# Sixteen products of ones instead of ten at the start of a fused attention, soft-MoE and GLU kernel, and another order for its attention stage

## The chip, the core and the metric

The kernel runs on one core of one Trainium2 chip. The core has TensorE (matrix products, called PE in the profile, with its weight loads as PEld), VectorE (DVE), ScalarE (ACT), GpSimd (POOL) and SyncE (SP), which here only issues DMAs. Each engine runs its own instruction list in order and waits for the others by semaphores. The metric is the device time of one launch in microseconds (us), as the median over runs. Before the change it is 510.9 us over 3 runs (509.9 to 510.99).

## The reference

Three layers follow each other, all in float32:

- causal attention over `q, k, v` of shape (4, 12, 448, 64): scores times 1/8, mask above the diagonal, softmax, times `v`. The result is laid out as `x` of 1792 tokens by 768;
- a soft mixture of 8 experts: `logits = x @ phi` (32 slots, 4 for each expert); softmax over the tokens gives the input of each slot, `d.T @ x`; each expert computes `relu(slot @ w1) @ w2` on its 4 slots (768 to 1024 to 768); softmax over the slots mixes the 32 results back to the tokens, `c @ slot_out`;
- a gated layer: `sigmoid(x @ w_gate) * (x @ w_val) @ w_out` (768 to 1536 to 768).

The weights of the experts are 50 MB, those of the gated layer 14 MB.

## The kernel before, in words

**Attention (0 to some 217 us).** The 48 heads are taken in 24 pairs; two pairs share one of 12 groups of loads (`q`, `k`, `v` of four heads, on SP's queue; the first `k` on ACT's). For a pair `i` the steps are: `T` (TensorE turns the rows of `q` and `k` into columns, tile `psT`), `hi` (ACT) and `lo` (DVE), which split them into two float16 parts (`qT`); `S` (scores in three products, `psS`), `m` (DVE: mask and row minimum), `e` (ACT: exponential, `P`), `pt` (TensorE transposes `P` into `psP`), `C` (ACT or DVE copies it to `PT`), `V` (times `v`, `psV`), `xu`, `Xa`, `xn` (back to rows), and for two pairs together `Y`, `yt`, `U`, `Ur`, `Ul` (logits; `Ul` is POOL's sum into `ln`). After each six pairs a tail (`psl`, `bm`, `eT`, `pse`, `A`, ...) folds the batch into the running softmax over the tokens. The scale of a group comes from its sums of squares: for groups 2 to 11 POOL squares (`sq`, two halves for `q` and two for `k`) and adds up in five halving steps (`add`, tiles `sq` and `sqr`), then TensorE spreads the sums over the partitions (`psq`) and DVE makes the scale (`sc`), which `hi` needs. In groups 0 and 1 DVE and ACT do the squares.

In the same stretch the first two weights of the gated layer are loaded and converted from their 64-bit words (`cv`: for each of six blocks two steps on ACT and two on DVE, tiles `w` and `first`), and expert weights are loaded ahead into nine buffers.

**The order is planned at build time.** `Plan` (L20 to L98) holds every step with its engines and an assumed length. `play` first goes backwards and gives each step a due time: that of its successor, less the successor's length times `slack`, less `margin`. Then it adds a constant for each kind of step from the table `SHIFT`. Then it goes forwards: of the steps that can start on the engine that is free first, within `wait` of the earliest, it issues the one with the smallest due time. What it issues is fixed: `on.te` and the rest (`Pinned`) keep the engines' program order. So at run time an engine never overtakes; it waits for the step that the plan put next. The times of the plan are not seen by the chip.

**Products of ones.** `keep_warm` (attention) multiplies a 128x128 tile of ones by two copies of itself into a spare bank (`psf`), and nobody reads it. The steps `("fs", n)` issue two such products each; they have an earliest time in the plan (`first=`) and a due time, so they are put where TensorE would be idle in the plan. `NFIRST` is their number. More products of ones (`("fl", k)`) stand in the last tail and ahead of the gated layer.

**Experts (217 to some 297 us).** The expert weights come in on SP's queue in tiles of 1.5 MB, four for each expert. Attention's memory is given back tile by tile, and five more buffers for weights (`w2p`, `w2px`) lie there. TensorE takes the experts in turn (`psh`, `psht`, `so`).

**Gated layer (to the end).** Six units of 256 columns, ordered by a second `Plan` with its own numbers (`SLACK`, `MARGIN`, `WAIT`, `GSHIFT`).

Of the kernel before, what the change touches and what calls it, by code (L numbers as in the profile page):

```python
# [19 lines left out]
class Plan:  # L20
# [5 lines left out]
    def op(self, key, f, on, deps=(), new=(), use=(), behind=(), due=1e9, first=0.0, lag=0.0, mode=""):  # L26
        for r, x in new:
            self.tiles[x] = [len(self.ops)]
        for x in use:
            self.tiles[x].append(len(self.ops))  # L30
        n = SimpleNamespace(key=key, f=f, on=on, deps=[self.at[x] for x in deps], new=list(new),
                            behind=[self.at[x] for x in behind], due=due, first=first, lag=lag, mode=mode, end=None, e=None)
        self.at[key] = len(self.ops)
        self.ops.append(n)

    def chained(self, x, key):
        was = self.last.get(x)
        self.last[x] = key
        return [was] if was else []
# [62 lines left out]
def kernel(  # L102
# [14 lines left out]
    B, H, S, D = q.shape  # L117
# [19 lines left out]
    for b in range(B):  # L137
        h = 0
# [5 lines left out]
    for g, (b, h0, n) in enumerate(GRP):  # L144
        for o in range(0, n, 2):
# [12 lines left out]
    NV = 2  # L158
    E0 = 6
    NH = 8  # L160
    NFIRST = 25
    LAND = (2.0, 5.5, 9.5)
    LDT = 3.9
    SLACK, MARGIN, WAIT = 0.213, 0.838, 0.347
# [22 lines left out]
    NFILL = 20  # L187
    AE = 9
    SQN = 32
    ASLACK, AMARGIN, AWAIT = 0.573, 1.325, 0.083  # L190
    PERIOD = 7.8
    SHIFT = {('A', 0): -67.34, ('A', 1): 96.11, ('C', 0): 69.6, ('C', 1): 119.07, ('C', 2): 112.34, ('C', 3): 125.19,
# [9 lines left out]
             3): -174.56, ('mr',): -54.03, ('p4',): -1.12, ('phi',): -95.42, ('pse',): -29.83, ('psl',): 20.96,  # L202
# [4 lines left out]
    XNB = 6  # L207
    PB = (0, 4, 2, 2)

# [5 lines left out]
    first = bctx.enter_context(tc.tile_pool(name="first", side="right", bufs=1)).tile([128, 2, KC, UC], F32, name="first")  # L215
# [123 lines left out]
    with ExitStack() as actx:  # L339
# [23 lines left out]
        P = {(t, h): P_p.tile([128, 128 * (t + 1)], F32, name=f"P{t}{h}") for t in range(NQ) for h in range(2)}  # L363
# [37 lines left out]
        xu = [x_p.tile([128, 512], F32, name=f"xu{n}") for n in range(2)]  # L401
        yt = x_p.tile([128, 512], F32, name="yt")
# [405 lines left out]
        op = pa.op  # L808
        plain = lambda f, *a: lambda e: f(*a)
# [142 lines left out]
                        k += 1  # L952

        for n in range(NFIRST):
            op(("fs", n), plain(keep_warm, n, 2), {"P": 0.21}, [], first=3.0 + 0.28 * n if n < 5 else 6.6 + 0.33 * (n - 5), new=[] if n else [("p", ("fs",))], use=[("fs",)] if n else [],
               behind=[("fs", n - 1)] if n else [])
        for n in range(NC + NA + NV):
            op(("w", n), lambda e: load_w(), {"D": 1.3}, [("cv", n - NC - NA, z, 3) for z in range(3)] if n >= NC + NA else [], lag=6.5,
               first=19.0 + 15.3 * n)
# [4 lines left out]
        for g_ in range(NG):  # L964
            group(g_)
            for i in range(2 * g_, 2 * g_ + 2):
                pair(i)
                if i % NPB == NPB - 1:
                    tail(i // NPB)
        pa.shift = SHIFT  # L970
        pa.play()
# [120 lines left out]
    for e in range(E):  # L1092
        if e == 0:
            hm = hm0
        else:
            ps = ps1.tile([128, 256], F32, tag="a", name="psh")
            for kc in range(KC):
                w = wt["1", e, kc // 3]
# [3 lines left out]
            hm = hm_p.tile([128, 256], F32, tag="hm", name="hm")  # L1102
            relu_own(hm, ps, e)
        pt = ps1.tile([128, 2, 128], F32, tag="b", name="psht")
# [4 lines left out]
        for f in range(8):  # L1109
            g, i = divmod(f, 2)  # L1110
            w = wt["2", e, f // 4]
# [4 lines left out]
        if e < B:  # L1116
# [3 lines left out]
            c = call[:, b]  # L1120
# [20 lines left out]
    pt = ps1.tile([128, 2, 96], F32, tag="b", name="psst")  # L1141
# [84 lines left out]
    op, chained, last = pl.op, pl.chained, pl.last  # L1226
# [37 lines left out]
    first = len(pl.ops)  # L1264
    prep(0)
    for n in range(NFILL):
        op(("fl", n), lambda e, n=n: keep_warm(n), {"P": 0.11}, [("fl", n - 1)] if n else [(psg, 0)], new=[] if n else [("o0", ("fl",))],
           use=[("fl",)] if n else [], due=10.0)
# [3 lines left out]
    for u in range(NU):  # L1272
        if 0 < u < NU - 1:
            prep(u + 1)
        for b in range(B):
            for c in range(2):
# [7 lines left out]
                   use=[("hs",) + k])  # L1284
# [3 lines left out]
        for i in range(TT):  # L1288
            bs = sorted({t // S for t in (128 * i, 128 * i + 127)})
            k = (u, i)  # L1290
            c = 1.95
            now += c + 0.51
            los, his = ([(f, b, u, c_) for b in bs for c_ in range(2)] for f in (hlo, hhi))
            new = [("o0", ("o0",) + k), ("o1", ("o1",) + k)]
# [5 lines left out]
            else:  # L1300
                op((outp,) + k, lambda e, k=k: outp(*k), {"P": c}, los + ([(wlo, u)] if u else []),
                   new=new, use=[("hid", b, u) for b in bs], behind=chained("out", (outp,) + k), due=now)
            for n in range(2):
                call = lambda f, n=n, k=k: lambda e: f(*k, n, *([e] if f is evict else []))
                e = {"A": 0.5, "V": 0.53} if u == 0 else {"A": 0.5} if u < NU - 1 and (n == 0 or i % 3 == AE and u < 4) else {"V": 0.53}
                a = u > 0 and "A" in e
# [40 lines left out]
```

## Time and profile before

| what | value |
|---|---|
| median of 3 runs | 510.9 us (509.9 to 510.99) |
| the profiled execution, own time | 510.54 us |
| its span, first to last instruction | 508.7 us |
| PE busy | 475.8 us (94%) |
| DVE, ACT, POOL busy | 379.8, 340.3, 283.7 us |
| mean granted TensorE clock | 0.989 |

An engine's busy share is a mean over three stages with different limits, so the stages are read one by one. Matrix products are pipelined and their ends are modelled: neighbours overlap in the rows, and the time from one start to the next tells the pace. A row of the timeline gives the start, the time from the first start to the last end, the engine, the line, the operation, the tiles and the number of instructions merged; in brackets is the idle time before it and who ended it. SPq and ACTq are the issues of DMAs. Nearly all instructions carry line 248, the helper `Pinned`, so they are told apart by their tiles.

### The profile page before, as it was taken

What the parts mean: (1) busy time and instruction counts of PE and PEld (TensorE: products, weight loads), DVE (VectorE), ACT (ScalarE), POOL (GpSimd) and SP (SyncE); (2) the same over time, 40 slices, a digit from 0 to 9 for tenths busy, and PEclk for the clock granted to TensorE, in tenths of its full rate; (3) what the DMA queues carried; (4) which work ended last, traced back from release to release, by engine and by line L of the source; (5) the groups of instructions that cost most, each with busy time, mean ns of one, the idle gap of its engine ahead of it and who ended that gap; (6) DMA issues with size and microseconds to landing.
All of it is one profiled execution on the core that took longest, in us unless ns stands there. A gap on an engine that the chain in (4) does not pass through costs nothing.

```text
span 508.7 us, 12285 instructions
## 1 busy us (share of the span) xinstructions
PE 475.8 (94%) x4614; PEld 297.9 (59%) x4614; DVE 379.8 (75%) x928; ACT 340.3 (67%) x772; POOL 283.7 (56%) x372
## 2 busy tenths in 40 slices
PE   8999999999999999999874678999999999999996
PEld 6676766677676767665441334555555555555553
DVE  4889999999999998522106039897998998988564
ACT  4899998888887977301131049899878989677410
POOL 3179778778878832000000005548799898998610
PEclk9999999999999999999995999999999999999999
DMA  9766685567765556789999995450353610200144
GB/s 189 195 155 198 184 225 133 162 200 209 212 147 161 167 162 251 300 341 414 421 421 421 412 398 222 171 201 1 125 206 118 247 51 1 91 35 1 57 193 186
DMA packets 84796, 101.56 MB, mean 200 GB/s; under 512 B 65024, under 2 KB 66176, under 8 KB 82688
## 3 DMA queue, kind: packets, MB, share of 16 engines
q1 hardware_dynamic: 84256, 100.32, 58.4%
q8 instruction: 36, 0.59, 0.5%
q10 hardware_dynamic: 480, 0.46, 0.3%
q14 instruction: 24, 0.20, 0.1%
HBM read 95.26 MB, written 5.51 MB: 198 GB/s over the span
## 4 chain that ended last, share of the span: by engine, by line
PE 56%; POOL 15%; DVE 9%; DMA 7%; ACT 6%; issue 5%; SPq 1%; POOLq 0%; ACTq 0%; DVEq 0%
PE pso L248 16%; PE psP L248 6%; PE psS L248 6%; PE psV L248 6%; POOL hlo L248 5%; DMA w<-in_moe_w_dram 5%; POOL sq L248 5%; POOL oacc L248 5%; PE so L1113 4%; PE psT L248 4%; PE psh L1100 3%; PE psY L248 2%; DVE psS L248 2%; PE psX L248 2%; PE psg L248 2%
## 5 line engine op out<-in xcount | busy, mean ns | idle before, releaser
L248 POOL TENSOR_TENSOR hlo<-hs,hhi 128x448 f16<-128x448 f32 x48 | 71.7, 1504 | 111.6 <-ACT hhi L248 111.2
L248 PEld LDWEIGHTS <-hhi 128*128 128x128 f16 x672 | 64.9, 98 | 50.2 <-issue 7.2
L248 ACT ACTIVATE P<-psS,nm 128x384 f32<-128x384 f32 (+3 forms) x168 | 82.2, 507 | 17.1 <-DVE nm L248 13.8
L248 PE MATMUL pso<-wh,hhi 128*128 128x384 f16 x336 | 83.1, 326 | 1.1 <-DVE oacc L248 0.4
L248 PE MATMUL pso<-wl,hhi 128*128 128x384 f16 x336 | 82.4, 326 | 0.0
L248 POOL TENSOR_TENSOR oacc<-oacc,ev 128x384 f32<-128x384 f32 x56 | 75.9, 1371 | 10.8 <-ACT ev L248 10.6
L248 PE MATMUL pso<-wh,hlo 128*128 128x384 f16 x336 | 81.4, 326 | 0.0
L248 DVE SCALAR_TENSOR_TENSOR w<-w 128x1536 int32<-128x1536 int32 (+1 forms) x36 | 69.3, 1926 | 0.4 <-ACT w L248 0.3
L248 DVE CUSTOM_DVE_ANT_0 psS<-psS,cmaskq,sc 128x128 f32<-128x128 f32 (+2 forms) x144 | 62.9, 488 | 1.9 <-PE psS L248 1.2
L248 DVE SCALAR_TENSOR_TENSOR oacc<-pso,osc,oacc 128x384 f32<-128x384 f32 x84 | 49.7, 611 | 18.5 <-PE pso L248 18.3
L248 POOL TENSOR_TENSOR sq<-sq 112x512 bf16<-112x512 bf16 (+1 forms) x80 | 55.3, 691 | 6.3
L248 ACT ACTIVATE w<-w 128x1536 int32<-128x1536 uint16 (+3 forms) x42 | 57.3, 1382 | 1.3 <-DMA w<-in_moe_w_gate_dram 1.3
L248 PE MATMUL psP<-ident,P 128*128 128x128 f32 x384 | 54.6, 278 | 0.3 <-ACT PT L248 0.3
L248 PEld LDWEIGHTS psP<-ident,P 128*128 128x128 f32 x384 | 42.0, 141 | 14.0 <-DVE nm L248 3.5
L248 PE MATMUL psS<-qT,qT 64*64 64x256 f16 (+3 forms) x1008 | 48.3, 287 | 0.7 <-ACT P L248 0.4
L248 PE MATMUL psV<-PT,v 128*64 128x448 f32 (+3 forms) x384 | 46.8, 386 | 0.0
L248 PEld LDWEIGHTS <-hlo 128*128 128x128 f16 x336 | 32.8, 98 | 23.6 <-POOL hlo L248 1.6
L248 ACT COPY PT<-psP 128x512 f32<-128x512 f32 x67 | 38.8, 600 | 3.7 <-PE psP L248 2.6
L248 ACT ACTIVATE ev<-pso,osc 128x384 f32<-128x384 f32 x56 | 32.3, 580 | 13.3 <-PE pso L248 9.6
L337 DVE TENSOR_SCALAR hm<-psh,emask 128x256 f32<-128x256 f32 x8 | 5.3, 663 | 45.8 <-PE psh L1100 43.3
L248 PEld LDWEIGHTS psV<-PT,v 128*64 128x64 f32 x384 | 25.4, 136 | 22.5 <-issue 14.0
L1108 ACT COPY hT<-psht 128x256 f32<-128x256 f32 x8 | 3.0, 372 | 50.6 <-PE psht L1106 43.8
(229 smaller groups left out, 863.6 us busy)
## 6 DMA issues: line engine op xcount, KB each, us to landing
w<-in_moe_w_dram SPq DMA_DIRECT2D x31, 1536.0 KB, 10.3
w<-in_moe_w_val_dram SPq DMA_DIRECT2D x6, 1536.0 KB, 10.7
w<-in_moe_w_gate_dram SPq DMA_DIRECT2D x6, 1536.0 KB, 6.6
w<-in_moe_w_out_dram SPq DMA_DIRECT2D x6, 1536.0 KB, 14.1
out_dram<-oacc SPq DMA_DIRECT2D x13, 384.0 KB, 2.3
k<-in_k_dram SPq DMA_DIRECT2D x44, 112.0 KB, 3.8
q<-in_q_dram SPq DMA_DIRECT2D x44, 112.0 KB, 3.4
v<-in_v_dram SPq DMA_DIRECT2D x36, 128.0 KB, 3.3
```

Of the source, the lines that this page charges most:

```text
L248: x = f(*a, **kw)
L337: nc.vector.tensor_scalar(to.rearrange("s (i q) -> s q i", i=2), ps.rearrange("s (q i) -> s q i", i=2), 0.0, emask[:, e:e + 1], ALU.max, A ...
L1100: nc.tensor.matmul(ps[32 * g:32 * g + 32, :], lhsT=slotT[:, kc, :], rhs=w[:, kc % 3, 256 * g:256 * g + 256], start=kc == 0, stop=kc == KC - 1)
L1108: nc.scalar.copy(hT, pt)
L1113: nc.tensor.matmul(so[32 * c:32 * c + 32, :], lhsT=hT[:, i, 32 * g:32 * g + 32], rhs=w[:, f % 4, 256 * c:256 * c + 256], start=e == 0 and ...
```

## The change

Three things change in the source.

1. `NFIRST` goes from 25 to 28, and the `fs` steps have other earliest times: the first eight (before: five) stand at 2.1 + 0.28 n us of the plan (before: 3.0 + 0.28 n), the other twenty at 6.6 us and every 0.33 us from there, as before. Each step issues two products, so sixteen instead of ten stand ahead of the first `T`.
2. The three numbers that steer attention's plan: `ASLACK`, `AMARGIN`, `AWAIT`.
3. The table `SHIFT`, nearly every entry, with the kinds `("c", 4)` added and `("e", 1)` and `("ld", 2)` dropped.

The steps, their assumed lengths, their dependencies and the buffers stay. The gated layer's plan and numbers stay. No step is added but the six products.

```diff
-    NFIRST = 25
+    NFIRST = 28
...
-    ASLACK, AMARGIN, AWAIT = 0.573, 1.325, 0.083
+    ASLACK, AMARGIN, AWAIT = 1.506, 2.13, 0.08
     PERIOD = 7.8
-    SHIFT = {('A', 0): -67.34, ('A', 1): 96.11, ('C', 0): 69.6, ('C', 1): 119.07, ('C', 2): 112.34, ('C', 3): 125.19,
...
-             152.24, ('c', 0): -12.82, ('c', 1): -9.48, ('c', 2): -10.23, ('c', 3): 64.35, ('cv', 0): -62.16, ('cv',
-             1): -28.45, ('cv', 2): 30.33, ('e', 0): -34.97, ('e', 1): -15.43, ('e', 2): 35.49, ('e', 3): 38.11,
-             ('eT',): -1.33, ('en',): 18.63, ('fl',): 61.86, ('fo',): 29.75, ('fs',): 8.52, ('h',): 21.02, ('hi', 0):
...
-             ('psq', 0): 5.55, ('psq', 2): -1.83, ('psq',): -70.09, ('pt', 0): -171.81, ('pt', 1): 89.79, ('pt', 2):
...
+    SHIFT = {('A', 0): -19.86, ('A', 1): 77.08, ('C', 0): 101.58, ('C', 1): 233.14, ('C', 2): 176.59, ('C', 3): -0.44,
...
+             ('bm',): 6.26, ('c', 0): -41.99, ('c', 1): -134.23, ('c', 2): -5.01, ('c', 3): 40.02, ('c', 4): 2.74,
+             ('cv', 0): -20.38, ('cv', 1): -0.86, ('cv', 2): 17.78, ('e', 0): -0.36, ('e', 2): 112.83, ('e', 3):
+             50.65, ('eT',): -9.25, ('en',): -16.92, ('fl',): 83.37, ('fo',): -9.93, ('fs',): 4.09, ('h',): 18.53,
...
+             0.02, ('mr',): -17.55, ('p4',): -37.61, ('phi',): 92.15, ('pse',): 9.98, ('psl',): -4.74, ('psq', 0):
+             22.0, ('psq', 2): -40.02, ('psq',): 160.93, ('pt', 0): 36.44, ('pt', 1): -25.77, ('pt', 2): 158.6, ('pt',
...
         for n in range(NFIRST):
-            op(("fs", n), plain(keep_warm, n, 2), {"P": 0.21}, [], first=3.0 + 0.28 * n if n < 5 else 6.6 + 0.33 * (n - 5), new=[] if n else [("p", ("fs",))], use=[("fs",)] if n else [],
+            op(("fs", n), plain(keep_warm, n, 2), {"P": 0.21}, [], first=2.1 + 0.28 * n if n < 8 else 6.6 + 0.33 * (n - 8), new=[] if n else [("p", ("fs",))], use=[("fs",)] if n else [],
                behind=[("fs", n - 1)] if n else [])
```

## Rows read from the trace of the kernel before

**Rows 1.** The page's busy times: engine, us, share of the span, instructions.

```profile
PE 475.8 (94%) x4614; PEld 297.9 (59%) x4614; DVE 379.8 (75%) x928; ACT 340.3 (67%) x772; POOL 283.7 (56%) x372
```

**Rows 2.** Stages: window, length, busy us by engine, granted clock, DMA share, GB/s.

```profile
25.00:50.00 25.00, 25.00 (x299) 17.12 (x295) 23.60 (x71) 24.12 (x71) 21.15 (x35) 1.00 0.68 180
...
225.00:235.00 10.00, 10.00 (x134) 5.38 (x131) 2.71 (x8) 1.44 (x3) 0.00 (x0) 1.00 1.03 431
...
270.00:280.00 10.00, 5.89 (x51) 2.44 (x50) 5.29 (x9) 2.11 (x4) 0.00 (x0) 0.54 1.02 423
280.00:300.00 20.00, 13.89 (x181) 7.26 (x182) 2.64 (x7) 1.33 (x4) 0.00 (x0) 1.00 1.01 409
...
400.00:508.00 108.00, 103.84 (x651) 59.94 (x649) 83.88 (x129) 64.78 (x103) 76.09 (x58) 1.00 0.26 96
```

**Rows 3.** Chain of waits that ended last, 190 to 330 us: start, us, what.

```profile
206.23 1.76 PE psV L248 x14
...
217.66 2.73 PE psh L248 x48
...
269.29 25.04 DMA w<-in_moe_w_dram
```

**Rows 4.** SP's queue, 217 to 221 us.

```profile
219.16 1.67 SPq L248 DMA_DIRECT2D w<-in_moe_w_dram  x2
```

**Rows 5.** Stages again, 4 us each, around the end of attention.

```profile
212.00:216.00 4.00, 3.62 (x64) 2.69 (x63) 2.69 (x12) 1.04 (x5) 0.58 (x2) 1.00 1.02 421
216.00:220.00 4.00, 4.00 (x60) 3.01 (x62) 1.60 (x6) 0.00 (x0) 0.00 (x0) 1.00 0.60 250
```

**Rows 6.** Timeline of the first 24 us, all engines.

```profile
1.16 2.31 PE L248 MATMUL psf<-ones 128*128 128x256 bf16 x10 [1.16 <-POOL ones L234]
...
4.56 1.76 PE L248 MATMUL psT<-ident,q 112*64 112x112 f32 x16 [1.08 <-DMA q<-in_q_dram]
...
6.37 1.76 PE L248 MATMUL psT<-ident,k 112*64 112x112 f32 x16
...
7.24 0.61 ACT L248 ACTIVATE qT<-psT,qks 128x448 f16<-128x448 f32 x1
...
8.06 1.46 PE L248 MATMUL psf<-ones 128*128 128x256 bf16 x6
8.17 0.63 ACT L248 ACTIVATE qT<-psT,qks 128x448 f16<-128x448 f32 x1 [0.32 <-PE psT L248]
...
8.84 0.68 DVE L248 SCALAR_TENSOR_TENSOR qT<-psT,qks,qT 128x448 f16<-128x448 f32 x1 [0.23 <-ACT qT L248]
...
9.38 1.08 PE L248 MATMUL psf<-ones 128*128 128x256 bf16 x8
...
10.39 1.26 PE L248 MATMUL psS<-qT,qT 64*64 64x256 f16 x30
...
11.58 0.99 PE L248 MATMUL psT<-ident,k 112*64 112x112 f32 x16
```

**Rows 7.** Stages of 8 us, 20 to 212 us: the sum over them.

```profile
sum 192.00, PE 189.07 PEld 132.78 DVE 176.18 ACT 160.10 POOL 132.15; mean PE 7.88 PEld 5.53 DVE 7.34 ACT 6.67 POOL 5.51
```

**Rows 8.** TensorE's waits, 17 to 217 us: total us, times, longest.

```profile
PE psq L248 <- POOL sqr L248: 1.6, 3, 0.6
PE psS L248 <- ACT P L248: 0.4, 1, 0.4
```

**Rows 9.** Timeline, 46.9 to 50.9 us: POOL's adds and a conversion on DVE.

```profile
46.94 3.80 POOL L248 TENSOR_TENSOR sq<-sq 112x512 bf16<-112x512 bf16 x4
...
47.38 1.27 DVE L248 SCALAR_TENSOR_TENSOR first<-w 128x512 int32<-128x512 int32 x1
```

**Rows 10.** Timelines: the same adds at 75.5 us; PE behind those at 46.94.

```profile
75.52 2.80 POOL L248 TENSOR_TENSOR sq<-sq 112x512 bf16<-112x512 bf16 x4
...
51.11 0.19 PE L248 MATMUL psq<-sqr,avgb 112*128 112x64 bf16 x1 [0.53 <-POOL sqr L248]
```

**Rows 11.** DVE's conversions: ns min/median/max, first and last start us.

```profile
L248 DVE SCALAR_TENSOR_TENSOR w<-w x6: 668/868/1266, 40.5 to 83.9; 128x512 int32<-128x512 int32 x6
L248 DVE SCALAR_TENSOR_TENSOR first<-w x6: 808/1032/1267, 47.4 to 91.9; 128x512 int32<-128x512 int32 x6
```

More of the change, by code (lines that the diff above doesn't have):

```diff
@@ L189 @@
     SQN = 32
-    ASLACK, AMARGIN, AWAIT = 0.573, 1.325, 0.083
+    ASLACK, AMARGIN, AWAIT = 1.506, 2.13, 0.08
     PERIOD = 7.8
-    SHIFT = {('A', 0): -67.34, ('A', 1): 96.11, ('C', 0): 69.6, ('C', 1): 119.07, ('C', 2): 112.34, ('C', 3): 125.19,
[9 rows of a table removed]
-             3): -174.56, ('mr',): -54.03, ('p4',): -1.12, ('phi',): -95.42, ('pse',): -29.83, ('psl',): 20.96,
[4 rows of a table removed]
+    SHIFT = {('A', 0): -19.86, ('A', 1): 77.08, ('C', 0): 101.58, ('C', 1): 233.14, ('C', 2): 176.59, ('C', 3): -0.44,
[9 rows of a table added]
+             0.02, ('mr',): -17.55, ('p4',): -37.61, ('phi',): 92.15, ('pse',): 9.98, ('psl',): -4.74, ('psq', 0):
[4 rows of a table added]
     XNB = 6
```

18 rows, old and new, of the table SHIFT are left out of this document.

## The prediction

> **What bounds the kernel now.** I read the page's busy times first, then the table of stages, then the chain of waits, and last the timeline of the one stage that the edit touches. The busy times put TensorE at 94% of the span [rows 1]; the reader is not to stop there, since the stages differ [rows 2]. In attention TensorE is busy all the time (25.00 of 25 us from 25 to 50 us). Among the experts it is not: from 270 to 300 us it is busy for 19.8 of 30 us while the DMA engines move 409 to 423 GB/s at a share of 1.0, and the chain names a transfer of expert weights there, 25.04 us long [rows 2, 3]. In the gated layer TensorE is the bound again (103.84 of 108 us).
>
> The question is whether attention's end reaches the end of the kernel through the stretch that the DMA bounds. It does. The stream of weights has a hole just where attention ends: the share is 1.02 from 212 to 216 us and 0.60 from 216 to 220 us, because buffers come free only when the first expert's product `psh` (217.66 us) has read them; the next two issues stand at 219.16 us [rows 3 to 5]. From there the stream is without a hole, its bytes are given, and the gated layer starts when it is through. So a microsecond won ahead of 217 us is a microsecond won at the end, and one lost is lost. In the hole the DMA engines stood for 40% of 4 us, 1.6 us: up to that much, the transfers ahead of it do not stop an earlier start either.
>
> **The change part by part.**
>
> *The six more products.* Ten products of ones take 2.31 us, from 1.16 us on, and TensorE then stands until the first rows of `q` have landed, 4.56 us, with 1.08 us of idle [rows 6]. The pace is 2.31/10 = 0.23 us or a little less for each, so six more take 1.39 us at most: sixteen end at 3.47 + 1.39 = 4.86 us, 0.30 us after the first `T` starts now. Products overlap by their ends, so the delay of `T` lies between 0 and 0.30 us; I take 0.1, because the next product does not wait for the last one's end. The cover for the other 1.1 us is the idle before `T`; if `q` landed earlier, all of the six would count.
>
> What they may bring stands in the same rows. Six products of ones at 8.06 us take 1.46 us, eight of the same at 9.38 us take 1.08 us; sixteen products of `T` take 1.76 us at 4.56 and at 6.37 us and 0.99 us at 11.58 us [rows 6]. [...] The granted clock reads 1.00 in attention [rows 2]; of the opening the durations tell more. TensorE had worked without a stop since 4.56 us when the pace rose, and the stop before it was that 1.08 us. The change closes this stop: work is then unbroken from 1.16 us, 3.4 us sooner. If unbroken work is what raises the clock, the rise comes up to 3.4 us earlier, near 6 us, and the second `T` (6.37 us) already runs in 0.99 us instead of 1.76.
>
> The working with an early rise: the second `T` ends near 6.4 + 0.1 + 0.99 = 7.5 us instead of 8.13. Its `hi` on ACT then waits no longer for `T` but for the `hi` ahead of it, 7.24 + 0.61 = 7.85 us, where it starts at 8.17 us now: 0.32 us. The second `lo` on DVE, 8.84 to 9.52 us now, is next: its predecessor on DVE ends at 8.61 us (7.93 plus 0.68 of its like), so it starts 0.23 us sooner and ends near 9.3 us. The first scores could start there. At present they could start at 9.5 us but start at 10.39, because the fourteen products of ones ahead of them (2.4 us at mixed pace) are not through [rows 6]. At the upper level fourteen take some 14 x 1.08/8 = 1.9 us from 7.5 us on, to 9.4 us, and the scores start near 9.4 us: 1.0 us sooner. Up to 17 us the later steps hang on each other through ACT and DVE, with more products of ones between, so most of it should pass on. I take 0.9 us gained, with the bounds +0.3 (the clock rises no sooner, `T` later by the whole 0.30) and -1.8 (a second score step freed in the same way: 2 x 0.9).
>
> [...]
>
> *The order.* Lengths and steps stay, so TensorE's work is the same, and a new order can only change its idle time and the hidden stalls between unlike products. In the 192 us from 20 to 212 us TensorE is idle for 192.00 - 189.07 = 2.9 us [rows 7]. More than half is one kind: `psq` waits for POOL's sums three times, 1.6 us in all [rows 8]. Order alone could win at most about those 2.9 us and a little of what the modelled ends hide, and it could lose as much or more. I take 0.8 us gained, half of what `psq` waits, and for this reason: the larger `AMARGIN` and `ASLACK` bring every step's due time forward by 0.8 us and 0.93 of a length more for each step behind it, so the long chains (load, squares, sums, `psq`, scale, `hi`, `lo`, scores) gain most against short ones, and POOL's sums are the chain that is late now. The table of shifts covers this with up to 280 us of its own for single kinds, and of those I can say no sign. Bounds: -4 (all 2.9 us and a third more hidden in stalls) and +4 (the mirror of it).
>
> The other edits of the table (the converted weights, the loads of weights, which have earliest times of their own, and `phi`) are costed at nothing: ACT, DVE and POOL have 192 - 160.10, 192 - 176.18 and 192 - 132.15 us free in the same stretch [rows 7]. DVE's 16 us are thin cover, and the first rival below takes them away.
>
> *Sum.* -0.9 - 0.8 = -1.7 us on the profiled execution's 510.54 us gives 508.8. That execution lies 0.4 us under the median of the runs, so the median comes to 509.2 us.
>
> **The rivals.**
>
> *Slower: the sums of squares come late more often.* Four of POOL's adds take 2.80 us at 75.52 us and 3.80 us at 46.94 us; in the second case a conversion on DVE, `first<-w`, lies over them, itself 1.27 us where the shortest of these takes 0.668, and `psq` is then idle for 0.53 us [rows 9 to 11]. Of ten `psq` three wait now [rows 8]. If the new order lays the twelve conversions over more of the adds, or puts `psq` further ahead on TensorE's list, those that now come free also wait: six more at 0.6 us are 3.6 us, and 510.54 - 0.9 + 3.6 = 513.2, as a median 513.6 us. It decides from the point at which more than four `psq` wait beyond today's three (4 x 0.6 = 2.4, more than the 0.9 of the start by over 1 us). Against it: the conversions are only 12, all between 40 and 93 us, and seven of ten sums are in time. For it: the table moves `psq` by up to 231 us and gives no word of POOL's real pace.
>
> [...]
>
> *No gain at the start.* The clock rises as late as now, or ACT and DVE, which the early scores then wait for, give the time back before 20 us. The start is then worth 0 and the order is small: 510.0 to 511.8 us as a median, at 510.9 without either. For it: from 11 to 17 us products of ones still fill TensorE, so it is not what is late there.
>
> *The order is worth more.* If most of the 2.9 us go and the stalls between unlike products shrink as well, -3.5 and -0.9 give 506.1, as a median 506.5 us.
>
> *The change does not do what it says.* The first eight steps could stand partly behind the first `T`; then the stop stays and it is the no-gain case.
>
> **How the numbers follow.** A measurement of this kernel can tell about 0.2%, 1.0 us: faster is under 509.9 us, slower over 511.9. The forecast (508 to 510 us) gets 0.40, of which 0.37 is faster; the larger gain 0.13; no gain 0.20; the slower case 0.27. That is 0.50 faster, 0.23 the same, 0.27 slower. The range reaches from the larger gain with a little more, 505.5, to just under the slower case's price, 513.3; about 0.1 is left out on each side.
>
> **What would show each step.** The opening timeline: sixteen `psf` in a row from 1.16 us, no idle of more than 0.1 us ahead of the first `psT`, which starts by 4.9 us; the second `psT` in about 1.0 us instead of 1.76; the first `psS` near 9.4 us. If the second `psT` still takes 1.76, the clock step is wrong. TensorE's waits: less than 1.6 us for `psq`, and a sum of idle under 2.9 us. The chain: `psh` near 216 us instead of 217.66, and everything behind it moved by the same amount; if `psh` moves and the end does not, the step through the DMA stretch is wrong. The prediction as a whole is wrong if `psh` starts later than now.

## The result and the profile after

The changed kernel takes 506.47 us (median of 6 runs, 505.29 to 508.5) against 510.94 us beside it: a ratio of 0.9917, 95% interval [0.9896, 0.9937], 4.2 us (3.2 to 5.3) faster. The forecast was 509.2 us, so the sign was right, the time lies in the range, and the size is more than twice what the sum gave. The profiled execution took 506.52 us with a span of 504.7 us.

The busy times of the page after; the line answers to [rows 1].

```profile
PE 474.2 (94%) x4620; PEld 297.6 (59%) x4620; DVE 369.9 (73%) x919; ACT 346.6 (69%) x781; POOL 283.6 (56%) x372
```

TensorE has six products more and is busy 1.6 us less; DVE is busy 10 us less and ACT 6 us more: of the 96 copies into `PT` the new plan gives DVE 7 instead of 29 and ACT the rest, and DVE's conversions are 2.0 us shorter, as will be seen. The opening, TensorE's lines of the timeline after, against [rows 6]:

```profile
1.16 3.59 PE L248 MATMUL psf<-ones 128*128 128x256 bf16 x16 [1.16 <-POOL ones L234]
...
4.69 1.05 PE L248 MATMUL psT<-ident,q 112*64 112x112 f32 x16
...
5.92 0.99 PE L248 MATMUL psT<-ident,k 112*64 112x112 f32 x16
...
8.63 0.30 PE L248 MATMUL psS<-qT,qT 64*64 64x256 f16 x4
...
9.20 1.15 PE L248 MATMUL psS<-qT,qT 64*64 64x256 f16 x26 [0.27 <-DVE qT L248]
```

The sixteen products run to 4.75 us without a stop, the first `T` starts 0.13 us later than before, and both `T` run at a faster pace, 1.05 and 0.99 us instead of 1.76 each. The scores start at 8.63 us and go on in earnest at 9.20, instead of 10.39.

TensorE's waits from 17 to 217 us after, and the sum over 20 to 212 us in stages of 8 us, against [rows 7, 8]:

```profile
PE psq L248 <- POOL sqr L248: 0.5, 1, 0.5
PE psS L248 <- ACT P L248: 0.4, 1, 0.4
```

```profile
sum 192.00, PE 190.65 PEld 135.29 DVE 169.35 ACT 165.38 POOL 131.81; mean PE 7.94 PEld 5.64 DVE 7.06 ACT 6.89 POOL 5.49
```

TensorE's idle time in attention is 1.35 us instead of 2.9; `psq` waits once instead of three times. The chain of waits after, against [rows 3]:

```profile
201.96 1.81 PE psV L248 x16
...
213.43 2.73 PE psh L248 x48
...
265.20 25.08 DMA w<-in_moe_w_dram
```

The first expert's product stands at 213.43 us instead of 217.66, 4.23 us sooner, and the long transfer at 265.20 instead of 269.29, 4.09 us sooner. What attention won reached the end through the stretch that the DMA bounds (share 1.02 and 403 to 427 GB/s from 270 to 300 us; execution 4.0 us shorter), and its hole is still there, somewhat smaller (the stage from 212 to 216 us, against [rows 5]):

```profile
212.00:216.00 4.00, 4.00 (x61) 2.78 (x60) 1.41 (x5) 0.00 (x0) 0.00 (x0) 1.00 0.71 265
```

All 4.2 us were won ahead of 213 us. A row on the tile `psV` splits them. It gives the shortest, median and longest product in ns, then the first and the last start in us; here before, then after.

```profile
L248 PE MATMUL psV<-PT,v x384: 219/379/591, 23.5 to 207.7; 128*64 128x448 f32 x48, 128*64 128x320 f32 x48, 128*64 128x192 f32 x48, 128*64 128x64 f32 x48
```

```profile
L248 PE MATMUL psV<-PT,v x384: 219/379/591, 22.4 to 203.5; 128*64 128x448 f32 x48, 128*64 128x320 f32 x48, 128*64 128x192 f32 x48, 128*64 128x64 f32 x48
```

The first `V` comes 1.1 us sooner: that is the opening. From the first to the last `V` it is 184.2 us before and 181.1 after (taken before rounding): 3.1 us, and that is the order of everything between. The forecast had 0.9 and 0.8 for these two. These are single executions; how far they vary is told with the experiments.

### The profile page after: what moved, and what is told of

Read it like the earlier page. It is cut to its first block, busy times and chain, and to the rows that moved or that the text cites. A ratio compares the mean times of both kernels' runs of the same rounds, so it can differ in the third digit from the quotient of the medians.

```text
span 504.7 us, 12336 instructions
## 1 busy us (share of the span) xinstructions
PE 474.2 (94%) x4620; PEld 297.6 (59%) x4620; DVE 369.9 (73%) x919; ACT 346.6 (69%) x781; POOL 283.6 (56%) x372
## 4 chain that ended last, share of the span: by engine, by line
PE 67%; POOL 10%; DMA 7%; DVE 6%; ACT 5%; issue 4%; SPq 1%; ACTq 0%; DVEq 0%; POOLq 0%
PE pso L248 17%; PE psP L248 9%; PE psV L248 8%; PE psS L248 8%; DMA w<-in_moe_w_dram 5%; POOL hlo L248 5%; PE so L1113 4%; PE psT L248 4%; POOL oacc L248 4%; PE psh L1100 3%; PE psX L248 2%; PE psY L248 2%; PE psg L248 2%; DVE w L248 1%; DMA w<-in_moe_w_gate_dram 1%
## 5 line engine op out<-in xcount | busy, mean ns | idle before, releaser
L248 ACT ACTIVATE P<-psS,nm 128x256 f32<-128x256 f32 (+3 forms) x168 | 82.9, 517 | 7.9 <-DVE nm L248 6.6
L248 ACT COPY PT<-psP 128x512 f32<-128x512 f32 x89 | 51.1, 595 | 9.0 <-PE psV L248 5.1
L248 POOL TENSOR_TENSOR sq<-sq 112x512 bf16<-112x512 bf16 (+1 forms) x80 | 52.9, 662 | 6.3
L248 PE MATMUL psP<-ident,P 128*128 128x128 f32 x384 | 56.3, 278 | 0.0
L248 PEld LDWEIGHTS <-hlo 128*128 128x128 f16 x336 | 32.8, 98 | 23.6 <-POOL hlo L248 1.6
```

Source lines behind the costliest of these rows:

```text
L248: x = f(*a, **kw)
```

## The experiments

Each kernel was timed against the kernel before on the same chip; a ratio of 0.998 is 1.0 us. "First to last `V`" is taken from the starts in the row shown above, before rounding, and is that of one execution. The whole list first:

| kernel | ratio to before, 95% interval | first `V`, us | first to last `V`, us |
|---|---|---|---|
| after, again | 0.9936 [0.9920, 0.9952] | 22.3 | 181.1 |
| before's order, sixteen products | 1.0006 [0.9987, 1.0024] | 22.3 | 183.8 |
| the same again | 0.9998 [0.9981, 1.0014] | 22.1 | 185.0 |
| after's order, ten products | 0.9955 [0.9938, 0.9972] | 22.7 | 180.4 |
| new table, old planning numbers | 1.0246 [1.0227, 1.0266] | 22.4 | 195.6 |
| before's order, no conversions on DVE | 0.9954 [0.9939, 0.9969] | 25.4 | 180.7 |
| after's order, no conversions on DVE | 0.9926 [0.9906, 0.9946] | 22.9 | 180.0 |
| before's order, four of five adds left out | 0.9923 [0.9905, 0.9942] | 22.9 | 180.4 |
| after's order, four of five adds left out | 0.9910 [0.9885, 0.9934] | 22.2 | 180.5 |
| before's order, one-operand conversions | 0.9916 [0.9897, 0.9936] | 23.6 | 180.9 |
| after's order, one-operand conversions | 0.9915 [0.9892, 0.9938] | 21.9 | 180.6 |
| before's order, one-operand conversions, sixteen products | 0.9881 [0.9855, 0.9907] | 22.5 | 180.4 |

**The two parts, one by one.** The changed kernel again, and each part alone:

> The changed kernel itself, on the same chip as the three runs beside it. Both theories: some 4.4 us under the kernel before (ratio 0.991), as the yardstick for the other three.

> The order of before to the last instruction, with six more products of ones ahead of the first T. Theory A (the early clock is worth about 1 us by itself, whatever the order): 0.9 us under before, 0.5 to 1.4, with the second psT in about 1.0 us instead of 1.76 and the first psS of pair 0 some 1 us sooner. Rival B (the start's gain of 1.1 us at the first psV comes from the new order of the opening, its phi load and products moved): within 0.3 us of before.

```diff
-plain(keep_warm, n, 2)
+plain(keep_warm, n, 2 if n else 8)
```

> The order of after, with ten products of ones ahead of the first T instead of sixteen. Theory A: some 0.9 us over the changed kernel (0.5 to 1.4), still 3.5 us under before. Rival B: within 0.3 us of the changed kernel. If it loses more than 2 us, the two parts are not independent.

```diff
-plain(keep_warm, n, 2)
+plain(keep_warm, n, 0 if n in (1, 2, 3) else 2)
```

TensorE's opening with before's order and sixteen products is that of after within 0.06 us:

```profile
1.16 3.60 PE L248 MATMUL psf<-ones 128*128 128x256 bf16 x16 [1.16 <-POOL ones L234]
4.68 1.02 PE L248 MATMUL psT<-ident,q 112*64 112x112 f32 x16
...
5.94 0.99 PE L248 MATMUL psT<-ident,k 112*64 112x112 f32 x16
...
9.26 1.15 PE L248 MATMUL psS<-qT,qT 64*64 64x256 f16 x26 [0.31 <-DVE qT L248]
```

The changed kernel gains 3.3 us this time, against 4.2 in the first measurement. Rival B fell at the opening: the products alone, not the new order there, make the early pace and bring the first `V` from 23.5 to 22.3 us. (With ten products in after's order it is 22.7 us: there the pace rose sooner than in the execution before, six products of ones at 7.91 us taking 0.83 us against 1.46 at 8.06 [rows 6], and the scores start at 9.57 us instead of 10.39.) At the end theory A is not shown: by the ratio the time is that of before (1.0006), by the medians 0.4 us less. In after's order the same six products are worth 507.73 - 506.72 = 1.0 us by the medians, and the order alone, with ten products, 2.3 us (ratio 0.9955). By the point values the parts do not add up: 0 and 2.3 against 3.3 to 4.2 together. Their intervals (from 1.2 us lost to 0.7 gained, and 1.4 to 3.2 gained) allow it all the same. The section on the start below asks whether before's order gives the start back.

**The reason given for the order.**

> The changed kernel with the three planning numbers of before (0.573, 1.325, 0.083) and the new table of shifts: another order again. The reason given in the prediction (the larger margins bring the long chain of POOL's sums forward) expects the order's gain mostly gone, 2 us or more over the changed kernel, with psq waiting for POOL's sums over 1.2 us in all. Its rival (the order is fitted as a whole, and the margins by themselves say nothing of POOL) expects psq's waits not to follow the time: psq may wait 0.5 us or less and the kernel still be 1 us or more slower.

```diff
-    ASLACK, AMARGIN, AWAIT = 1.506, 2.13, 0.08
+    ASLACK, AMARGIN, AWAIT = 0.573, 1.325, 0.083
```

It is 12.5 us slower than before. Its two longest waits are no sums of squares:

```profile
PE psX L248 <- DVE xu L248: 2.7, 1, 2.7
PE psV L248 <- ACT PT L248: 2.2, 3, 0.9
PE psq L248 <- POOL sqr L248: 2.1, 3, 1.1
```

`psq` waits over 1.2 us, as the forecast's reason wanted, but it is one of nine kinds of wait in the list. The table belongs to its planning numbers, and the run does not tell what the numbers do by themselves. The opposite pair, the new numbers with the old table, was not tried: that plan comes to a point at which every step waits for a buffer. This test of the reason stays inconclusive.

**What in the order.** Two suspects were taken out of both orders in turn, all else in its place: the conversions on DVE, then POOL's adds.

> The order of before, with DVE's twelve conversion steps of the first two weights left out (their target is set to zero by GpSimd at the start, so unit 0 of the gated layer computes on zeros). Theory C (the conversions collide with POOL's adds in before's order and make both late, which the new order avoids): 2 us under before (1.3 to 3), idle of TensorE from 44 to 76 us down from 1.7 us to under 0.7. Rival D (TensorE's own sequence, the stalls between unlike products and inside them, is what the order changed): under 0.7 us, and the same for both orders.

> The same with the order of after. Theory C: 0.5 us or less under the changed kernel, so the distance between the two orders shrinks by 1 to 2.5 us against the full pair. Rival D: the distance between the orders stays within 0.7 us.

```diff
-            elif m == 2:
-                ve.scalar_tensor_tensor(lo, hi, -2 ** 31, lo, ALU.bitwise_and, ALU.bitwise_or)
-            else:
-                ve.scalar_tensor_tensor(w32[nm, 0][:, x].bitcast(I32), hi, 3, lo, ALU.logical_shift_left, ALU.bitwise_or)
...
+        nc.gpsimd.memset(first, 0.0)
```

> The order of before, with POOL's first four halving adds of the sums of squares left out (40 tiles of 2 x 4 adds; the scales of groups 2 to 11 then come from a part of the squares). POOL is never late. Theory E (POOL's late sums are what the order mended: 1.6 us of direct waits of psq and more behind them): 1.6 us or more under before, up to 3. Rival D: under 0.8 us.

> The same with the order of after. Theory E: 0.5 us under the changed kernel or less, so that the distance between the orders shrinks by over 1 us. Rival D: both orders gain alike, within 0.5 us of each other.

```diff
-            m = 2 * HG * D
+            m = SQN
             while m >= SQN:
```

Without the conversions before's order gains 2.4 us although its opening is late in that run (first `V` at 25.4 us: the zeroing on GpSimd comes ahead of the first scale, and TensorE's pace is still low at 11.8 us, where it had risen by 9.53 us before), and after's order gains nothing that can be told from 0.9917 to 0.9936. Without the adds (80 in all) before's order gains 3.9 us, more than the 1.6 to 3 expected, and after's 0.4 to 1.3 us against its own two ratios. From first to last `V` both orders then take the same: 180.4 and 180.5 us without adds, 180.7 and 180.0 without conversions, against 184.2 and 181.1. TensorE's idle time from 44 to 76 us, which theory C wanted under 0.7 us, is 1.74 us before and 0.00 without the conversions. Theories C and E hold in their direction, rival D falls: TensorE's own sequence is not what makes the difference. Leaving out either one of the two suspects is enough to remove it, which points to the pair. Both edits also take work away, the adds some 51 us of POOL's, so a third kernel keeps the work.

**Hold-up or work.** The conversion steps read two operands from SBUF. A step of the same shape with one operand takes the second read away and leaves DVE nearly the same time (0.63 to 0.68 us, against 0.64 and 0.69 for the two-operand steps beside which nothing of POOL's runs, in before's order without the adds). The operation and the data type change with it:

> The order of before, to the last instruction, with the twelve conversion steps on DVE replaced by a step of the same shape that reads one operand from SBUF instead of two (a maximum over an axis of length one; the sign and the low bits of unit 0's weights are then lost). DVE still works some 0.67 us for each. Theory F (what hurts is that a two-operand step and POOL's adds hold each other up): nearly all that leaving the steps out gave, 2 us under before (1.3 to 2.8), the adds down from 55.3 us to about 51.5 and no step longer than 0.75 us. Rival G (it is DVE's work as such, 8 us in a stretch where DVE has no time to spare): 0.7 us or less under before, with the adds hardly shorter.

> The same with the order of after. Theory F: within 0.6 us of the changed kernel, so that the distance between the two orders is 1 us or less beyond what the start gives. Rival G: the distance between the orders stays at 2 to 3 us beyond the start.

```diff
-                ve.scalar_tensor_tensor(lo, hi, -2 ** 31, lo, ALU.bitwise_and, ALU.bitwise_or)
+                ve.tensor_reduce(lo.bitcast(F32), hi.bitcast(F32).rearrange("p a (b o) -> p a b o", o=1), axis=AX.X, op=ALU.max)
             else:
-                ve.scalar_tensor_tensor(w32[nm, 0][:, x].bitcast(I32), hi, 3, lo, ALU.logical_shift_left, ALU.bitwise_or)
+                ve.tensor_reduce(w32[nm, 0][:, x], hi.bitcast(F32).rearrange("p a (b o) -> p a b o", o=1), axis=AX.X, op=ALU.max)
```

The ratios are 0.9916 and 0.9915: by their times the two orders are equal. Before's order gains 4.3 us (3.3 to 5.3), more than the 1.3 to 2.8 expected: as much as the whole change, and with ten products only. DVE keeps the 29 copies into `PT` in it, so handing copies to ACT is not needed for the gain. Theory F holds in its direction, rival G falls. The rows of the conversions after, and those of the one-operand steps in before's order, against [rows 11]:

```profile
L248 DVE SCALAR_TENSOR_TENSOR w<-w x6: 683/694/1109, 37.2 to 80.0; 128x512 int32<-128x512 int32 x6
L248 DVE SCALAR_TENSOR_TENSOR first<-w x6: 682/748/1060, 38.1 to 88.3; 128x512 int32<-128x512 int32 x6
```

```profile
L248 DVE TENSOR_REDUCE w<-w x6: 634/674/681, 40.7 to 81.3; 128x512 f32<-128x512 f32 x6
L248 DVE TENSOR_REDUCE first<-w x6: 630/655/678, 47.5 to 88.3; 128x512 f32<-128x512 f32 x6
```

Before, the medians were 868 and 1032 ns; after, 694 and 748; with one operand, 674 and 655. POOL's adds by shape, 20 to 182 us (busy us and mean ns behind the bar), before, after, and with one-operand steps in before's order:

```profile
L248 POOL TENSOR_TENSOR sq<-sq 112x512 bf16<-112x512 bf16 x20 | 24.6, 1232 | 1.6
L248 POOL TENSOR_TENSOR sq<-sq 112x256 bf16<-112x256 bf16 x20 | 14.4, 719 | 1.6
```

```profile
L248 POOL TENSOR_TENSOR sq<-sq 112x512 bf16<-112x512 bf16 x20 | 23.6, 1179 | 1.6
L248 POOL TENSOR_TENSOR sq<-sq 112x256 bf16<-112x256 bf16 x20 | 13.4, 669 | 1.6
```

```profile
L248 POOL TENSOR_TENSOR sq<-sq 112x512 bf16<-112x512 bf16 x20 | 23.1, 1157 | 1.6
L248 POOL TENSOR_TENSOR sq<-sq 112x256 bf16<-112x256 bf16 x20 | 13.4, 669 | 1.6
```

Over all four shapes of adds it is 55.3, 52.9 and 51.1 us, and over the twelve conversions 11.6, 9.7 and 7.9 us. With the one-operand steps as the undisturbed length, the adds lost 4.2 us and the conversions 3.7 before, and 1.8 and 1.7 after. But POOL as a whole loses as much after as before. Its busy time on the page is 283.7 us [rows 1] and 283.6 us, and with one-operand steps, in before's order and in after's:

```profile
PE 474.5 (94%) x4614; PEld 298.0 (59%) x4614; DVE 376.5 (74%) x928; ACT 339.7 (67%) x772; POOL 279.5 (55%) x372
PE 475.4 (94%) x4620; PEld 298.5 (59%) x4620; DVE 369.7 (73%) x919; ACT 346.2 (68%) x781; POOL 279.8 (55%) x372
```

So POOL loses 4.2 us before and 3.8 after: in the new order 2.1 us of it (steps under a conversion, each against the median of its own shape) lie on other steps than the four adds. What the new order changes on POOL is which steps are held up, not how much. Which steps lie over each other is to be seen in the timeline. Before, each of the twelve conversions overlaps with one of POOL's squares or first four adds, one of them in [rows 9]; after, seven do, and five fall on other steps of POOL's, as here (after, 47.8 to 49.2 us; `first<-w` undisturbed at 0.68 us, and POOL's `r` of 0.24 us stretched to 0.66):

```profile
47.95 0.68 DVE L248 SCALAR_TENSOR_TENSOR first<-w 128x512 int32<-128x512 int32 x1
48.08 0.66 POOL L248 TENSOR_SCALAR r<-sum 128x7 f32<-128x7 f32 x1 [0.21 <-ACT P L248]
```

And the place of [rows 9] in before's order with one-operand steps: three conversions over the four adds, and nobody waits.

```profile
46.74 2.79 POOL L248 TENSOR_TENSOR sq<-sq 112x512 bf16<-112x512 bf16 x4
...
47.50 0.63 DVE L248 TENSOR_REDUCE first<-w 128x512 f32<-128x512 f32 x1
48.05 0.67 DVE L248 TENSOR_REDUCE w<-w 128x512 f32<-128x512 f32 x1
48.65 0.67 DVE L248 TENSOR_REDUCE first<-w 128x512 f32<-128x512 f32 x1
```

How the loss reaches TensorE can be followed product by product, since both kernels have the same order on TensorE. At 50 us they are level (0.1 us). The one-operand kernel is ahead by 0.6 us from `psq` at 51.1 us on, 1.3 from `psS` at 60.3, 2.2 from `psq` at 68.1, 2.6 from `psU` at 69.0, 3.3 from `psq` at 85.1 and 3.5 from `psS` at 94.6, and still by 3.25 at `psh` (214.41 us against 217.66). So all of it is won between 51 and 95 us, where the conversions are (40.5 to 93.1 us): 2.1 us at the three waits of `psq` and the rest at five smaller places near them. The first `psq` before stands in [rows 10]; here the other two, and then the first and the third of the one-operand kernel, which do not wait:

```profile
68.09 0.19 PE L248 MATMUL psq<-sqr,avgb 112*128 112x64 bf16 x1 [0.56 <-POOL sqr L248]
85.12 0.19 PE L248 MATMUL psq<-sqr,avgb 112*128 112x64 bf16 x1 [0.53 <-POOL sqr L248]
```

```profile
50.51 0.20 PE L248 MATMUL psq<-sqr,avgb 112*128 112x64 bf16 x1
81.87 0.19 PE L248 MATMUL psq<-sqr,avgb 112*128 112x64 bf16 x1
```

In [rows 9] a conversion takes 1.27 us and the four adds 3.80 us where they meet; with the one-operand steps it is 0.63 to 0.67 us and 2.79 us in the same place. The edit changes the second read, the operation and the data type together, and these runs do not show which of the three ends the hold-up.

**Where the start goes in before's order.**

> The kernel of the first run on the start once more (order of before, six more products of ones), since its answer (0.4 us by the medians, with an interval of 1 us to either side) and that of the opposite pair (1.0 us) differ. If the start is worth the same in both orders, 0.6 to 1.2 us under before; if before's order gives it back behind the opening, within 0.4 us.

> The order of before with the one-operand conversion steps (the sign and the low bits of unit 0's weights are lost, as there) and six more products of ones. Theory H (in before's order the start's gain of 1.2 us at the first psV is eaten by the same hold-ups between conversions and adds, which fall otherwise when everything starts earlier): without them the gain passes on, some 1 us under the one-operand kernel with ten products, that is 5 us under before (ratio near 0.990), and first psV to last psV takes 180.5 to 181 us as there. Rival I (before's order gives the start back for another reason, such as the loads' fixed pace): the same time as with ten products (ratio near 0.992), and first to last psV 1 us longer.

Both have the edit of the first run on the start, one on the two-operand and one on the one-operand steps of before's order:

```diff
-plain(keep_warm, n, 2)
+plain(keep_warm, n, 2 if n else 8)
```

The repetition gave 0.9998: by the ratios the start is worth nothing that can be measured there (over both, between 1.0 us gained and 1.2 us lost). By the medians it is worth 0.4 and 0.6 us; eight of the 24 runs lie over 1.2 us above their kernel's median. With the hold-ups gone the ratio is 0.9881 against 0.9916 with ten products, 1.8 us by the point values and 0.9 us by the medians of the two kernels (on two chips), but the intervals [0.9855, 0.9907] and [0.9897, 0.9936] overlap.

The traces do not bear theory H out. It wants some 1 us more from the first to the last `V` with sixteen products: that is 184.2 us with ten, and 183.8 and 185.0 with sixteen. In the 185.0 one wait is 1.26 us long, for which the profile shows no releaser; the kernel with 183.8 has no such wait:

```profile
137.35 0.97 PE L248 MATMUL psV<-PT,v 128*64 128x448 f32 x4 [1.26 <-issue]
```

From the first `T` on the order on TensorE is the same with ten and with sixteen. Compared product by product, the lead is 1.3 and 1.4 us at the first scores, and 1.2 and 1.3 us at 109 us, past all twelve conversions. So the hold-ups do not eat it, and `psh` starts 1.6 and 0.6 us sooner than before (217.66 us):

```profile
216.02 2.73 PE psh L248 x48
217.06 2.73 PE psh L248 x48
```

In after's order, where the times gave 1.0 us, it is the other way round. With ten products TensorE is 0.9 us behind at the first scores and no longer behind from 30 us on, and `psh` starts 0.45 us sooner than with sixteen (213.43 us). That execution is longer only behind attention: the gated layer's first `psg` comes 81.75 us after `psh` with ten products, and 79.32 us with sixteen. Here `psh` and `psg` with ten, then `psg` with sixteen:

```profile
212.98 2.73 PE psh L248 x48
294.73 1.55 PE psg L1036 x24
```

```profile
292.75 1.55 PE psg L1036 x24
```

So it is not shown that the start is worth more in one order than in the other. By the medians it is worth 0.4 to 1.0 us in all four pairs, by the ratios between nothing and 1.8, and these runs do not settle it.

## Why the prediction was right in sign and short in size

- **The bound and the way to the end** held in this pair. `psh` moved by 4.23 us, the DMA stretch by 4.09, the execution by 4.0. In other traces the stretch behind `psh` varies by up to 2.6 us, so single executions tell no more than that.
- **The cost of the six products** held: `T` is 0.13 us later (forecast 0.1, bound 0.30).
- **The early pace** held, and came sooner than worked out: the first `T` already takes 1.05 us instead of 1.76 in the profiled execution, where the forecast expected the faster pace for the second alone. What sets the rise no run shows: the 0.9 us was the author's estimate from [rows 6], on the condition that unbroken work raises the pace. What the runs showed is that it rises earlier with sixteen products (the second `T` takes 0.99 to 1.30 us) than with ten (1.72 to 1.76 us). First scores at 8.63 and 9.20 us against a forecast of 9.4, first `V` 1.1 us sooner against 0.9. The closeness is partly luck of the two executions: in the kernels without the zeroing on GpSimd the first `V` stands between 22.7 and 23.6 us with ten products and between 21.9 and 22.5 with sixteen.
- **That the start passes on** is not settled. By the medians it is worth 1.0 us in after's order and 0.4 and 0.6 in before's, by the ratios 1.0 and nothing. In the traces the lead reaches `psh` in before's order and is gone by 30 us in after's, so the rival of the time given back is not refuted.
- **The order** is the step that failed in size: "I take 0.8 us gained, half of what `psq` waits". It measured 2.3 us alone by the times (1.4 to 3.2), and in the traces between first and last `V` 3.1 us, or 3.9 with ten products in both orders. Of its parts one stays open and one was wrong. The reason, larger planning numbers that bring POOL's chain forward, is not shown by any run. And the conversions were "costed at nothing", with DVE's 16 us of idle as cover. They are the main term: in before's order all twelve lie over POOL's squares and adds and cost the adds 4.2 us and themselves 3.7. In the new order they cost the adds 1.8 and themselves 1.7, and the rest of POOL's loss falls on steps for which TensorE hardly waits. With the hold-ups gone and the order kept, TensorE is 3.5 us ahead behind the last conversion; 2.1 us of that lie at `psq`, which the forecast had at 0.8.
- **The slower rival** had the mechanism, with the right pair of engines and the right rows, and the wrong sign: in the new order seven conversions instead of twelve lie over squares or adds. It was priced in one direction only. The other, what before's own overlaps cost, stood in the rows that the prediction showed: six conversions at 868 ns and six at 1032 are 11.4 us [rows 11], where twelve at the shortest 668 ns are 8.0. Those 3.4 us on DVE, and what the adds lose beside them, are a price for a larger gain; whether the new order avoids the overlaps, the rows of before could not tell. That the result falls on the larger gain's 506.5 us, to which the prediction gave 0.13, is in part luck: that rival took most of the 2.9 us of idle time, and 1.6 us of it went.

## What to carry to other kernels

When an order planned with fixed lengths is redrawn, first list the steps whose length in the trace is far from their shortest (a median of 1032 ns where 630 is possible): here they met another engine. The new order is judged by what waits behind the steps that are held up: POOL lost 4.2 and 3.8 us in the two orders, and only one of them made TensorE wait. A term for such overlaps belongs in the sum with both signs. Where two kernels have the same order on the bounding engine, compare them instruction by instruction: it shows where a gain arises and where it ends, which two times 1 us apart do not.

## What the hardware showed that was not expected

The size of the hold-up: twelve conversions of 0.67 us, 8 us of DVE work in 200 us, and POOL's adds cost each other 7.9 us of engine time, and by that cost the kernel 4.3 us (ratio 0.9916). In after's order the hold-ups that are left, some 5.5 us of engine time (POOL 3.8, DVE 1.7), cost nothing that can be measured (0.9915 against 0.9917 and 0.9936).

The point at which TensorE's pace rises moves from run to run. Before, the products of ones start 0.21 us apart up to 9.10 us and 0.11 us apart from 9.53 us on. With ten products the second `T` still ran at the lower pace in all five kernels profiled (1.72 to 1.76 us). With sixteen it took 0.99 us in most and 1.16 and 1.30 us in two, where the rise fell into it, and the first `T` took anything from 0.99 to 1.76 us. Ahead of the rise the engine had worked without a pause like the 1.08 us of [rows 6]: from 1.16 us on with sixteen products, from 4.3 to 4.6 us on with ten. In the kernel with ten products and no conversions it paused once more, for 0.77 us up to 6.90 us, and the pace was still low at 11.8 us. A pause after the rise left the pace as it was in one execution: with sixteen products and no conversions TensorE stood for 1.22 us behind the first `T` (0.99 us), and the second `T` took 0.99 us as well.
